# A recurrent attention loop that streams weights: one place and one block a step fewer

## The chip, the cores and the metric

The kernel runs on one core of a Trainium2 chip. Its engines work side by side, each through its own instruction stream: TensorE (PE for its matmuls, PEld for its weight loads), VectorE (DVE), ScalarE (ACT), GpSimd (POOL) and SyncE (SP), which here only issues DMAs. Sixteen DMA engines move data between HBM and the on-chip memory SBUF. The metric is the device time of one execution in microseconds. A time is the median of the runs shown.

## The reference

Two independent parts are computed and their outputs put side by side.

Part A is attention with a recurrent memory. The sequence of 2048 rows of 1024 is cut into 64 segments of 32. Each step joins the 8 memory rows with its 32 rows to `h` (40 rows), and computes with the same four weight matrices (1024 x 4096 each, bf16, 8 MB):

```
q, k, v = h Wq, h Wk, h Wv            # 32 heads of 128
p = softmax(q k^T * scale, masked)    # memory keys are seen by all; key j is allowed if j <= i, or i < 8
o = (p v) Wo
mem = o[:8];  out = o[8:]
```

`mem` is the input of the next step, so the steps run one after the other.

Part B is a long convolution by a state-space model: a kernel of 2048 taps for each of 1024 channels, from exponentials and cosines of 128 states, applied by a Fourier transform (in this kernel by matmuls with sine and cosine matrices), plus `u * Dskip`.

## The kernel before, in words

Part B comes first (0 to about 718 us of the profile). Beside it, part A's work that doesn't depend on the memory is done ahead: 24 rows of every segment are transposed and stored (`XTd`), and the projections of its last 8 rows are computed and stored (`PKd`). While B runs its table loop, SyncE also copies the weight blocks that will be streamed into DRAM tiles of their own (`streamed_copies`, tiles `WD_...`), and loads a first part of the weights that will stay.

Then comes part A's loop, `part_a`, 64 steps over `s` (line 339). The four matrices are 64 blocks of 128 x 2048 (512 KB each): `(m, t, kc)` for k, q and v, with half `t` of the heads and row block `kc` of 0 to 7, and `("o", u)` with `u` of 0 to 15 for Wo. They don't all fit in SBUF:

- *resident* blocks (`RESIDENT`) are loaded once and stay,
- two blocks (`KEPT`) lie in PSUM, and VectorE copies them from there to SBUF in five pieces each every step (`fetch`, L282),
- the blocks of `STREAM` and `STREAM_O` are *streamed*: loaded again each step, into one of `SLOTS` places in turn (`unit`, line 254, load at L268, tile `wst`).

`unit(key)` is called in the order in which TensorE uses the blocks, and it writes the load of a streamed block into SyncE's queue at that point. What paces it is the place: load number n waits until TensorE has used the block of load n - SLOTS. SyncE works its queue strictly in order, so a waiting entry holds up all behind it. The other entries of a step are hung on a block by the dictionary `between`: `load_pk` (L312, what was computed ahead for this step), `load_xt` (L317, the rows of the next step), and the two stores of the step before (`stores`, L327 to `OLd`, L331 to the output).

TensorE's order in a step: k half 0, q half 0 (8 blocks each; L349, four matmuls a block), transposes L360, k half 1 in two halves, scores (L373 to L380), q half 1, v half 0, v half 1, the products with the probabilities (L417, L421), then Wo's 16 blocks (L448, eight matmuls a block) and the transposition of the new memory (L542), which VectorE copies into `hT` (L543). That copy begins the next step; its start is the zero of the "step's clock" in this text. ScalarE evicts (L355, L435, L361), VectorE does the softmax and the block-diagonal spreading of the probabilities (L387 to L406).

Two tiles share memory with others under one tag and make entries of SyncE's queue wait: `xt` has tag `F`, which `lb0b` has before it (read by TensorE at L421, in the product of half 0), and `pk` is used until the last L421 of a step.

In the first step, resident blocks that have no place yet are loaded by `unit` as they come up (`rest`, L223). After the last step, the rows that were left for later are multiplied by Wo once more (L571), for which the Wo blocks that are not resident are loaded again.

GpSimd's DMA descriptors lie in the first 4096 bytes of each SBUF partition (`SCRATCH`, line 1315), and `low_blocks` puts three resident blocks behind them.

Of the kernel before, what the change touches and what calls it, by code (L numbers as in the profile page):

```python
# [21 lines left out]

STREAM = {("k", 0): (1,), ("q", 0): (0, 6), ("k", 1): (3,), ("q", 1): (0, 5), ("v", 0): (2, 7), ("v", 1): (2, 7)}
STREAM_O = (4, 7, 10, 14)

KEPT = {("k", 0, 7): (("B", 0, 512), ("C", 512, 512), ("A", 1024, 512), ("F", 1536, 256), ("L", 1792, 256)),
        ("o", 15): (("B", 0, 512), ("C", 512, 512), ("E", 1024, 512), ("F", 1536, 256), ("L", 1792, 256))}
SLOTS = 5  # L30


def weight_blocks(Wq, Wk, Wv, Wo):
# [15 lines left out]
def streamed_keys():  # L49
    return [key for key in [(m, t, kc) for (m, t), kcs in STREAM.items() for kc in kcs] + [("o", u) for u in STREAM_O]]  # L50

# [175 lines left out]
def part_a(ctx, tc, x, src, WD, HE, seg_len, out_a, ahead, W_res, rest, places, first):  # L227
# [20 lines left out]

    loads = [SLOTS]


    between = {}

    def unit(key):
# [9 lines left out]
        if key in first:  # L264
            return first.pop(key)
        t_ = wst.tile([128, 2048], BF16, name="wst", tag="w%d" % (loads[0] % SLOTS))
        loads[0] += 1
# [13 lines left out]
    def words(out, in_):  # L281
        nc.vector.tensor_scalar(out=out.bitcast(I32), in0=in_.bitcast(I32), scalar1=0, scalar2=None, op0=ALU.bitwise_or)  # L282

    def load_kept(key):
        i = len(kept)
        if key in first:
            t_ = first.pop(key)
        else:
            t_ = wst.tile([128, 2048], BF16, name="wst", tag="w%d" % (loads[0] % SLOTS))
            loads[0] += 1  # L290
            nc.sync.dma_start(out=t_[:].rearrange("e (h d) -> e h d", h=2) if key[0] == "o" else t_[:], in_=src(key))
        kept[key] = [ps_k.tile([128, 512], F32, name="keep", tag="keep%d" % (2 * i + n)) for n in range(2)]
        for n in range(2):
            words(kept[key][n][:], t_[:, 1024 * n:1024 * n + 1024])

    def fetch(key):

        ahead_of[key] = []
        for tag, lo, n in KEPT[key]:
            t_ = work.tile([128, n], BF16, name="piece", tag=tag)  # L300
            words(t_[:], kept[key][lo // 1024][:, lo % 1024 // 2:(lo % 1024 + n) // 2])
            ahead_of[key].append((lo, n, t_))
# [7 lines left out]
    def load_pk(j):  # L310
        pk = pers.tile([128, 768], BF16, name="pk", tag="pk")
        nc.sync.dma_start(out=pk[:], in_=PKd[j])  # L312
        return pk
# [12 lines left out]
    def stores(s, ob):  # L326
        nc.sync.dma_start(out=OLd[s // 8][:, 256 * (s % 8):256 * (s % 8) + 256], in_=ob[:, 1, :])  # L327
        rows = out_a[s * SL:s * SL + SL, :].rearrange("r (q d) -> q r d", q=4)
        if s + 1 < NS:

            nc.sync.dma_start(out=rows, in_=ob[:, 0, :])  # L331
        else:
            for q in range(4):
                nc.sync.dma_start(out=rows[q][0:XM], in_=ob[32 * q:32 * q + XM, 0, :])

    load_kept(("k", 0, 7))
    fetch(("k", 0, 7))
    between["v", 0, 2] = lambda: load_kept(("o", 15))
    for s in range(NS):
        def quads(m, t, kcs, a=None):  # L340
            if a is None:

                pool, tag = {("q", 0): (ps_sc, "sc"), ("q", 1): (ps_pv, "pv")}.get((m, t), (ps_acc, "acc"))
                a = pool.tile([128, 512], F32, name="acc", tag=tag)
            for kc in kcs:
                w = unit((m, t, kc))
                for g in range(4):
                    for o_, rhs in columns(w, 512 * g, 512):
                        nc.tensor.matmul(a[32 * g:32 * g + 32, o_:o_ + rhs.shape[1]], lhsT=hT[:, kc, :], rhs=rhs,  # L349
                                         start=(kc == 0), stop=(kc == KC - 1), tile_position=(0, 32 * g), skip_group_check=True)  # L350
            return a
# [101 lines left out]


        pks = []
        between["q", 0, 6] = lambda: pks.append(load_pk(s))
        if s:
            between["q", 1, 0] = lambda: stores(s - 1, ob)
        a = quads("k", 0, range(KC))
        k0 = evac(a, "A")  # L460
        a = quads("q", 0, range(KC))
# [73 lines left out]
        ob = work.tile([128, 2, 256], BF16, name="ob", tag="E")  # L535
# [801 lines left out]
def kernel(  # L1337
# [34 lines left out]
    def residents(stay, early):  # L1372
# [26 lines left out]
        for _ in range(EARLY[1]):  # L1399
            load_resident(tc, pool, src, rest.pop(0), W_res)  # L1400
            yield
        for i, key in enumerate([("k", 0, 7)] + streamed_keys()[0:SLOTS - 1]):
            first[key] = t_ = ahead.wst.tile([128, 2048], BF16, name="wst", tag="w%d" % i)
# [25 lines left out]
    with ExitStack() as ctx_a:  # L1429
        part_a(ctx_a, tc, A_x[0], src, WD, A_Wo.shape[0] * A_Wo.shape[1], seg_len, out_a, ahead, W_res, rest, places, first)  # L1430
# [35 lines left out]
```

## Time and profile before

| | us |
|---|---|
| median of 3 runs (2254.4 to 2264.52) | 2254.61 |
| the profiled execution: its own time | 2254.61 |
| its span | 2252.9 |
| part A's loop, first L349 to last L448 | 718.6 to 2190 |
| mean distance of two copies into hT (63 of them) | 22.6 |
| TensorE busy in the span | 1965.9 (87%) |
| VectorE busy | 1466.7 (65%) |
| DMA share and rate, 900 to 2100 us | 0.93 to 0.94, 342 to 349 GB/s |

In profile lines, L268 is line 268 of the kernel. A line of a group gives line, engine, operation, tiles (written<-read), shapes and count, then busy time and mean; a line of waits gives who waited for whom, microseconds in all, times and the longest. SPq is SyncE's queue: an entry there is the issue of a DMA, not its transfer. The ends of matmuls are modelled and a little late, so that matmuls seem to overlap, and a wait of less than about 0.2 us doesn't show.

### The profile page before, as it was taken

To read this page: it belongs to the slowest core of one execution; us is meant where nothing else is said; L and a number is where in the kernel's file an instruction comes from. 1 tells how busy PE (TensorE), PEld (TensorE's weight loads), DVE (VectorE), ACT (ScalarE), POOL (GpSimd) and SP (SyncE) were. 2 spreads that over 40 slices of the span, in tenths; PEclk is the share of its full clock that TensorE was granted. 3 is DMA by queue.
4 is the path that set the end of the run, shared out by engine and by line. 5 is a ranking of instruction groups with operands and counts; after the bars stand their busy time and mean duration, and the time that the engine had idled before them with its cause. 6 is when DMAs were issued, how large, how long until landed. Compare 5 with 4: busy or idle time off the path is not lost.

```text
span 2252.9 us, 77860 instructions
## 1 busy us (share of the span) xinstructions
PE 1965.9 (87%) x33798; PEld 1174.4 (52%) x33798; DVE 1466.7 (65%) x3160; ACT 976.3 (43%) x1599; POOL 359.5 (16%) x623
## 2 busy tenths in 40 slices
PE   1699999879999788989989898999998988999889
PEld 1365666657887344444444444544444444444444
DVE  8599999989995456565656565656565656565640
ACT  6699999932323233333333333333333333333330
POOL 2154444556222000000000000000000000000020
PEclk9999999989999899999999999999999999999999
DMA  6777886667459999999999999999999999999991
GB/s 161 194 197 228 226 238 180 176 178 243 156 180 318 345 329 335 349 335 355 323 346 345 347 340 354 345 355 333 355 337 356 332 356 330 355 342 360 333 377 37
DMA packets 351883, 657.84 MB, mean 292 GB/s; under 512 B 118616, under 2 KB 209912, under 8 KB 349492
## 3 DMA queue, kind: packets, MB, share of 16 engines
q1 hardware_dynamic: 336324, 608.69, 77.3%
q0 software_dynamic: 15216, 44.18, 5.8%
q8 instruction: 264, 4.33, 0.8%
q14 instruction: 79, 0.65, 0.1%
HBM read 597.97 MB, written 66.31 MB: 295 GB/s over the span
## 4 chain that ended last, share of the span: by engine, by line
PE 35%; DVE 24%; DMA 23%; issue 9%; ACT 6%; SPq 2%; POOL 1%; DVEq 0%; ACTq 0%; POOLq 0%
PE acc L349 16%; DMA wst<-WD_q 12%; DMA wst<-WD_o 5%; PE pe L571 3%; PE tr L360 3%; PE pro L158 2%; DVE nr L1068 2%; DMA out_dram<-uu 2%; PE ups L866 2%; DVE sc L388 2%; DVE sc L395 2%; DVE mx L393 2%; PE pp L448 2%; DVE pt L397 2%; PE pa L1037 2%
## 5 line engine op out<-in xcount | busy, mean ns | idle before, releaser
L349 PEld LDWEIGHTS <-hT 128*32 128x32 bf16 x12352 | 322.8, 97 | 323.6 <-issue 107.0
L355 ACT CAST ev<-acc 128x512 bf16<-128x512 f32 x384 | 224.8, 585 | 347.1 <-PE acc L349 341.1
L349 PE MATMUL acc<-W,hT 128*32 128x512 bf16 x4864 | 370.7, 381 | 0.0
L349 PE MATMUL acc<-wst,hT 128*32 128x512 bf16 x2560 | 257.7, 384 | 17.7 <-DMA wst<-WD_q 14.4
L448 PEld LDWEIGHTS <-oT 128*32 128x32 bf16 x8192 | 202.5, 96 | 111.2 <-issue 85.0
L282 DVE TENSOR_SCALAR piece<-keep 128x256 int32<-128x256 int32 (+1 forms) x640 | 188.9, 360 | 40.1 <-PE pp L448 31.3
L349 PE MATMUL acc<-MF,hT 128*32 128x512 bf16 x2048 | 182.4, 383 | 0.0
L448 PE MATMUL pp<-W_o,oT 128*32 128x256 bf16 x4096 | 159.2, 275 | 14.0 <-DMA W_o<-in_A_Wo_dram 5.6
L368 POOL COPY KT<-pk 128x128 bf16<-128x128 bf16 x128 | 37.7, 294 | 828.6 <-PE acc L349 372.0
L361 DVE COPY KT<-tr 128x512 bf16<-128x512 bf16 x64 | 27.2, 424 | 215.1 <-PE tr L360 215.1
L387 DVE TENSOR_REDUCE mx<-sc 128x8 f32<-128x320 f32 x128 | 62.1, 485 | 159.3 <-PE sc L380 159.3
L435 ACT CAST oT<-pv 128x512 bf16<-128x512 f32 x128 | 75.0, 586 | 165.1 <-PE pv L421 162.6
L448 PE MATMUL pp<-wst,oT 128*32 128x256 bf16 x2048 | 102.6, 277 | 26.6 <-DMA wst<-WD_o 25.9
L158 PE MATMUL pro<-xTl,wsl 128*128 128x512 bf16 x512 | 120.2, 386 | 5.2 <-ACT xTl L102 5.2
L361 ACT COPY QT<-tr 128x512 bf16<-128x512 bf16 x128 | 75.0, 586 | 109.5 <-PE tr L360 107.9
L389 ACT ACTIVATE sc<-sc 128x320 f32<-128x320 f32 x128 | 54.0, 422 | 156.6 <-DVE sc L388 150.3
L1007 PEld LDWEIGHTS <-MF 128*128 128x128 bf16 x1024 | 102.6, 100 | 29.9 <-issue 8.5
L360 PEld LDWEIGHTS <-ev 128*128 128x128 bf16 x1024 | 57.9, 97 | 110.0 <-issue 80.6
L321 POOL COPY hT<-xt 128x192 bf16<-128x192 bf16 x63 | 21.9, 347 | 562.3 <-DMA xt<-XTd 473.9
L1007 PE MATMUL hps<-KT,MF 128*128 128x256 bf16 x720 | 94.3, 284 | 14.4 <-DVE x L1182 11.4
L1239 PE MATMUL yp<-Bt,MI 128*128 128x256 bf16 x680 | 102.8, 273 | 0.8 <-ACT yb L1255 0.8
L538 ACT CAST ob<-pp 128x128 bf16<-128x128 f32 x64 | 17.0, 265 | 197.8 <-DVE ob L537 197.8
(314 smaller groups left out, 3962.2 us busy)
## 6 DMA issues: line engine op xcount, KB each, us to landing
wst<-WD_q SPq DMA_DIRECT2D x256, 512.0 KB
wst<-WD_v SPq DMA_DIRECT2D x256, 512.0 KB
wst<-WD_o SPq DMA_DIRECT2D x256, 512.0 KB
wst<-WD_k SPq DMA_DIRECT2D x128, 512.0 KB
Ud<-ux POOLq DMA_DIRECT2D x16, 1024.0 KB, 5.6
uq<-Ud SPq DMA_DIRECT2D x32, 512.0 KB
pk<-PKd SPq DMA_DIRECT2D x64, 192.0 KB
wsl<-in_A_Wk_dram SPq DMA_DIRECT2D x16, 512.0 KB
```

What stands on the lines that cost most here:

```text
L158: nc.tensor.matmul(a[:], lhsT=w[:, kc, 128 * j:128 * j + 128], rhs=xTl[:, kc, :, :].rearrange("p s k -> p (s k)"), start=(kc == 0), stop=( ...
L282: nc.vector.tensor_scalar(out=out.bitcast(I32), in0=in_.bitcast(I32), scalar1=0, scalar2=None, op0=ALU.bitwise_or)
L349: nc.tensor.matmul(a[32 * g:32 * g + 32, o_:o_ + rhs.shape[1]], lhsT=hT[:, kc, :], rhs=rhs, start=(kc == 0), stop=(kc == KC - 1), tile_pos ...
L355: nc.scalar.copy(out=q[:], in_=a[:])
L360: nc.tensor.transpose(out=p[:, i, hl, :, :].rearrange("p a b -> p (a b)"), in_=q[:, 128 * hl:128 * hl + 128], identity=ident[:])
L361: eng(out=dst, in_=p[:, i, :, :, :])
L387: nc.vector.tensor_reduce(out=mx[:], in_=sc, axis=AX.X, op=ALU.max)
L435: nc.scalar.copy(out=o[:], in_=p[:].rearrange("p a (g q) -> p a g q", g=4))
L448: nc.tensor.matmul(po[32 * qt:32 * qt + 32, :], lhsT=oT[:, h % 4, (h % 16) // 4, :], rhs=columns(w, 1024 * hh + 256 * qt, 256)[0][1], star ...
L571: nc.tensor.matmul(pe[n][:], lhsT=left[2 * b + hi // 16][:, 128 * (hi % 16):128 * (hi % 16) + 128], rhs=wo[u][:, 1024 * hh + 512 * n:1024 ...
L1007: pe.matmul(s_[r][half][:, cs, :], lhsT=MF[:, kc, 4 * rr + mc, cs, :], rhs=rhs, start=(i == 0 and mc == 0), stop=(i == 1 and mc == 3), ski ...
L1239: pe.matmul(yp[:, b, :], lhsT=m_[:, b, cs, kc, :], rhs=Bt[:, kc, j, half, c_, :], start=(kc == 0 and cs == 0 and half == 0), stop=(kc == 3 ...
```

## The change

One place fewer for streamed blocks (four for five), and one block fewer streamed in a step (13 for 14), which becomes resident. Which blocks are streamed is chosen anew, and with that the places at which the other entries of SyncE's queue are hung. `SCRATCH`, `low_blocks` and all arithmetic stay.

```
-STREAM = {("k", 0): (1,), ("q", 0): (0, 6), ("k", 1): (3,), ("q", 1): (0, 5), ("v", 0): (2, 7), ("v", 1): (2, 7)}
-STREAM_O = (4, 7, 10, 14)
+STREAM = {("k", 0): (1,), ("q", 0): (1, 7), ("k", 1): (4,), ("q", 1): (1,), ("v", 0): (0, 4), ("v", 1): (0, 5)}
+STREAM_O = (3, 7, 10, 14)
...
-SLOTS = 5
+SLOTS = 4
...
-    between["v", 0, 2] = lambda: load_kept(("o", 15))
+    between["v", 0, 0] = lambda: load_kept(("o", 15))
...
-        between["q", 0, 6] = lambda: pks.append(load_pk(s))
+        between["q", 0, 7] = lambda: pks.append(load_pk(s))
         if s:
-            between["q", 1, 0] = lambda: stores(s - 1, ob)
+            between["k", 1, 4] = lambda: stores(s - 1, ob)
```

SyncE's queue over one step, from the load of xt on:

```
before: xt, o10, o14, k0.1, q0.0, pk, q0.6, k1.3, stores, q1.0, q1.5, v0.2, v0.7, v1.2, v1.7, o4, o7
after:  xt, o10, o14, k0.1, q0.1, pk, q0.7, stores, k1.4, q1.1, v0.0, v0.4, v1.0, v1.5, o3, o7
```

(q0.6 is block 6 of q, half 0; from k0.1 on they are for the next step.)

## The prediction

> **What bounds the kernel now.** I read the page first, for the stage in which the change lies. Slices are 56.3 us wide; the attention recurrence runs from about 719 us (first L349) to 2190 us.
>
> ```profile
> span 2252.9 us, 77860 instructions
> ...
> DMA  6777886667459999999999999999999999999991
> GB/s 161 194 197 228 226 238 180 176 178 243 156 180 318 345 329 335 349 335 355 323 346 345 347 340 354 345 355 333 355 337 356 332 356 330 355 342 360 333 377 37
> ...
> PE 35%; DVE 24%; DMA 23%; issue 9%; ACT 6%; SPq 2%; POOL 1%; DVEq 0%; ACTq 0%; POOLq 0%
> ```
>
> The DMA engines look full from slice 13 on, and DMA is 23% of the chain that ended last. That would make every megabyte less a gain. But a share of busy time is not a wait, so I asked next what TensorE itself waits for between 770 and 2160 us, some 62 steps that are alike (the view of waits, PE alone):
>
> ```profile
> PE tro L542 <- DVE ob L537: 27.4, 61, 0.5
> PE acc L349 <- DVE hT L543: 22.9, 61, 0.4
> PE pp L448 <- DMA wst<-WD_o: 18.9, 31, 1.6
> ...
> PE acc L349 <- DMA wst<-WD_q: 14.1, 33, 0.9
> ...
> PE acc L349 <- DMA wst<-WD_k: 2.3, 7, 0.6
> PE acc L349 <- DMA wst<-WD_v: 0.2, 1, 0.2
> ```
>
> Columns: microseconds in all, times, longest. Weights cost TensorE 18.9+14.1+2.3+0.2 = 35.5 us there, 0.57 us of a 22.6 us step (63 copies into hT, L543, from 760.8 to 2164.4 us). The rest is instruction stream and the turn of the state (L542, L543), which the change leaves alone. Then what SyncE's DMA queue waits for, in the same stretch, and one step of that queue in order of time:
>
> ```profile
> SPq L317 <- PE pv L421: 217.7, 62, 3.9
> SPq L327 <- ACT ob L545: 114.5, 61, 3.2
> SPq L312 <- PE pp L421: 100.7, 61, 2.1
> ```
>
> ```profile
> 1525.65 0.32 SPq L317 DMA_DIRECT2D xt<-XTd  x1
> 1526.02 1.82 SPq L268 DMA_DIRECT2D wst<-WD_o  x2
> 1527.94 0.39 SPq L268 DMA_DIRECT2D wst<-WD_k  x1
> 1528.42 0.38 SPq L268 DMA_DIRECT2D wst<-WD_q  x1
> 1530.21 0.32 SPq L312 DMA_DIRECT2D pk<-PKd  x1
> 1530.58 0.42 SPq L268 DMA_DIRECT2D wst<-WD_q  x1
> 1531.20 0.41 SPq L268 DMA_DIRECT2D wst<-WD_k  x1
> 1533.66 0.32 SPq L327 DMA_DIRECT2D OLd<-ob  x1
> 1534.03 0.55 SPq L331 DMA_DIRECT2D out_dram<-ob  x1
> 1534.67 1.11 SPq L268 DMA_DIRECT2D wst<-WD_q  x2
> ```
>
> Every step SyncE stands 217.7/62 = 3.5 us at the load of xt, which takes over the tile lb0b and so waits for L421 to have read it; Wo blocks 10 and 14 are queued behind. In this step the load before them landed at 1527.19 and theirs at 1530.67 and 1531.95 (the trace's landing records): between 1527.2 and the start of their packets the DMA engines run dry, some 2 us in every step. From there they work without a pause: landings 1.2 to 1.4 us apart at 1530.67, 1531.95, 1533.33, 1534.65, pk 1535.12. So what matters is not the bytes of a step but the chain that starts anew at xt. Where it is too late stands in TensorE's own timeline:
>
> ```profile
> 1531.99 0.40 PE L448 MATMUL pp<-wst,oT 128*32 128x256 bf16 x8 [0.19 <-DMA wst<-WD_o]
> ...
> 1537.50 0.40 PE L349 MATMUL acc<-wst,hT 128*32 128x512 bf16 x4 [0.27 <-DMA wst<-WD_q]
> 1537.71 0.40 PE L349 MATMUL acc<-MF,hT 128*32 128x512 bf16 x4
> ```
>
> The first is Wo block 14 (landed 1531.95), the second Wq block 6 of half 0 (landed 1537.45): they start 0.04 and 0.05 us after the landing.
>
> **The change part by part.** Times below are on a step's clock, zero at the copy into hT (1533.68 here), as medians of the 53 to 58 steps I could read whole.
>
> *Later places in q, half 0.* Streamed blocks 0 and 6 become 1 and 7. After xt the queue holds the same things in the same order: Wo 10, Wo 14, Wk 1, a Wq block, pk, a Wq block. Same bytes, so the last lands when it does now, at 3.8, and TensorE reaches it one block later: four matmuls, 0.22 us start to start (1537.71 less 1537.50 above is 0.21). A wait shrinks by 0.22 us at most; 33 waits of 14.1/33 = 0.43 us are mostly longer: 33 x 0.22 = 7.3 us. Taken from start to start (which also sees what the modelled ends hide) the wait is 0.37 us a step and would be 0.22: 0.15 x 63 = 9.5 us. I take 8.5. The first Wq block waits in one step in 58: 0.5 us at most. The later issue does no harm: block 1 goes out when Wo 7's place is free (-3.7), 6 us before its use at 2.3; block 7 when Wo 10's is (-2.5), 6.2 us before 3.7.
>
> *Wo.* Block 4 becomes 3, which feeds nothing that waits. Blocks 10 and 14 keep their place on TensorE and their place behind xt; with four places 14 also waits for the use of Wv 5 of half 1, over 0.5 us after L421, while SyncE comes to it 0.9 us or more after L421. Their 18.9 us stay: 0, bounds -18.9 and +10 (half as much again).
>
> *One block less a step, 14 to 13.* 1.3 us of DMA time. It goes missing in the stretch before xt, where the streamed v blocks and Wo 7 land 0.6 to 1.7 us before their use already; the dry time grows from 2 to about 3 us. 0. If it shortened the chain after xt, up to all of the remaining 35.5 us would go; that end goes to a rival.
>
> *Four places.* A load is now held back by the use four loads earlier. Laid out with today's block starts, the time from that use's end to the new block's use is 5.9 to 6.9 us, and 4.7 for Wo 10, which xt sets as now. A load that finds the engines idle took 1526.02 to 1530.67 = 4.65 us with a long issue, 4.1 in the median; one in a full queue 5.5 to 7.5. At one block per 1.69 us (22/13) against 1.3 us of transfer the queue drains between blocks, so 0; the one tight place comes next.
>
> *Stores moved ahead of Wk 4, half 1.* Today Wk 3 goes out before the two stores (1531.20). In the new order SyncE stands at the stores until ACT's copy L545 (-0.02), and Wk 4 goes out at 1.0 where Wq 0 of half 1 does now (1534.67). TensorE wants it at about 5.9 (Wk 3's median start 5.43, plus one transpose of 0.33 and two blocks less what was saved). Queued behind the late Wq 7 (3.8), the stores and its own 1.3 us it lands near 5.4: today's block there lands at 6.67 with Wk 3's 1.27 us more ahead of it. It is late in about 5 steps of 54; I take +2 us. Bounds: 0 (it lands 3.5 us after its issue, as Wo 10 does), and +47 us (it takes the 5.2 us after the end of its issue that today's block there takes, so lands at 6.64, 0.74 us late, 63 times).
>
> The trace has five landing records for each out_dram store and sixteen for each weight load. The Trainium skill, "DMA: Bandwidth & Descriptors", section "Why a DMA increments its semaphore by 16 and not by 1", says that a copy is spread over the largest count up to 16 that divides the slowest dimension of both sides; by it, with 4 column groups, the store sits on four engines, and Wk 4's share there stands behind 32 packets of 512 B instead of 8. At the trace's 27 ns a packet that is 0.65 us later, 6.05 instead of 5.4, and the sum would be some 10 to 15 us higher. Today's block after the same store lands 1.56 us after Wk 3, which leaves no room for it.
>
> *First step and the rest.* The list of resident blocks has 49 entries for 48; the loads before the loop are one streamed block fewer, those that the first step makes as it goes are 12 for 11. There SyncE issues block by block at 1.36 us (745.15 to 749.15, three and one) and TensorE stalls on each: +1.4 us. One copy fewer among the table work of the first stage, and the same five Wo blocks reloaded at the end: 0, within 2 us.
>
> **Sum:** -8.5 - 0.5 + 2 + 1.4 = -5.6 us. The profiled execution's own time is 2254.61 us (span 2252.9), equal to the median shown; so 2249.
>
> **Rivals.** *Both weight waits go.* If the chain after xt runs faster because fewer loads share the engines, the 33 (q) and 31 (Wo) waits vanish. For it: the block behind each is often late on one engine only. Against: the loads ahead are the same ones. Half of it, 2235; all, -35.5 + 1.4 with hidden parts, about 2215. *Slower: Wk 4 behind the stores.* Nothing hides it: it is used 4.9 us after its issue, and if it needs more than that the excess is paid 63 times. Loads at that place of the queue take 5.2 us after issue's end (4.3 to 5.6 for the middle 8 in 10). At 5.2, 2249 - 2 + 47 = 2294; at 4.8, about 2265. *It does nothing:* if Wq 7 also lands later by its place (it is issued half a microsecond later), the 8.5 us stay and the time is 2257; that lies in my own range.
>
> **How the numbers follow.** Small gain or nothing (2238 to 2258): 0.52. Waits go (2208 to 2238): 0.23. Wk 4 late, or four places too few elsewhere (2258 to 2305): 0.25. Leaving a tenth on either side: 2217 to 2288; the likeliest alone 2238 to 2258. Half a per cent, 11.3 us, is about what can be told from no change: below 2243.3 lie the second and a fifth of the first, 0.33; above 2265.9 most of the third, 0.23; between, 0.44.
>
> **What would show it.** Right: TensorE's wait for WD_q at about half of 14.1 us, for WD_o near 18.9, for WD_k under 5; the stall of L317 unchanged; the DMA share at about 0.88 for 0.93. Wrong: a wait for WD_k of tens of microseconds (the stores), waits for WD_v (four places), or WD_o's wait gone (the chain after xt was not what I took it for).

## The result and the profile after

The changed kernel takes 2296.4 us (median of four runs, 2295.36 to 2297.48), the kernel before 2256.81 in the same comparison (2254.4 to 2264.52). The ratio is 1.0169, 95% interval 1.0142 to 1.0196: slower by 40 us, where I had forecast 2249 and a range of 2217 to 2288. The profiled execution of the changed kernel has an own time of 2297.48 us, 42.9 more than the one of before.

From its page, the span, the two DMA rows of the 40 slices, and the shares of the chain that ended last:

```profile
span 2295.8 us, 77858 instructions
...
DMA  6777885666368988998899989899899899999991
GB/s 162 197 218 222 224 228 167 181 205 231 118 236 306 315 305 300 319 314 297 299 318 321 312 315 312 299 313 314 309 301 317 306 316 315 323 312 321 313 347 49
...
PE 42%; DMA 29%; DVE 11%; issue 8%; ACT 6%; SPq 1%; POOL 1%; ACTq 0%; DVEq 0%; POOLq 0%
```

In the loop (slices 13 to 37) the DMA engines move some 310 GB/s where they moved 345, and yet their share of the chain has grown from 23% to 29%. Fewer bytes, and TensorE waits for them longer. The view of waits, TensorE alone, 770 to 2200 us (the last copy into hT is now at 2207.5; columns are microseconds in all, times, longest):

```profile
PE pp L448 <- DMA wst<-WD_o: 29.3, 48, 1.9
PE tro L542 <- DVE ob L537: 27.3, 61, 0.5
PE acc L349 <- DVE hT L543: 22.9, 61, 0.4
PE acc L349 <- DMA wst<-WD_k: 22.0, 33, 1.7
...
PE acc L349 <- DMA wst<-WD_q: 12.0, 27, 1.2
...
PE acc L349 <- DMA wst<-WD_v: 1.0, 3, 0.4
```

The waits on the turn of the state (L542, L543) are what they were. The weights cost 64.3 us for 35.5: WD_k went from 2.3 to 22.0, WD_o from 18.9 to 29.3, and WD_q only from 14.1 to 12.0. SyncE's queue in the same stretch:

```profile
SPq L268 <- PE acc L349: 299.4, 327, 2.8
SPq L317 <- PE pv L421: 162.9, 62, 2.8
SPq L327 <- ACT ob L545: 135.8, 61, 3.6
```

It stands less long at xt (162.9 for 217.7 us), because it comes there later: with four places it has been held up by L268, the weight loads, before. All waits of the queue at L268, of which the first line is the largest, add up to 708 us, and to 475 in the kernel before (770 to 2160 us). One step of the queue and, below it, what TensorE does when Wk 4 of half 1 is due:

```profile
1535.92 0.98 SPq L268 DMA_DIRECT2D wst<-WD_q  x1
1538.02 0.32 SPq L327 DMA_DIRECT2D OLd<-ob  x1
1538.43 0.55 SPq L331 DMA_DIRECT2D out_dram<-ob  x1
1539.08 0.42 SPq L268 DMA_DIRECT2D wst<-WD_k  x1
1539.59 0.38 SPq L268 DMA_DIRECT2D wst<-WD_q  x1
```

```profile
1543.55 0.40 PE L360 MATMUL tr<-a_ident,ev 128*128 128x128 bf16 x4
1544.22 0.40 PE L349 MATMUL acc<-wst,hT 128*32 128x512 bf16 x4 [0.27 <-DMA wst<-WD_k]
1544.43 0.40 PE L349 MATMUL acc<-W,hT 128*32 128x512 bf16 x4
```

Wk 4 is issued behind the two stores, at 1539.08, and lands at 1544.18 by the trace's landing records; its first matmul starts 0.04 us later. In 29 of the 61 steps the profile shows a wait there (the other 4 of the 33 are at the first Wk block).

Where the 42.9 us came from, start to start, as means over the 59 steps that can be read whole (a step lasted 22.60 us before and 23.30 after, 0.70 more; over all 62 it is 0.67). From the first copy into hT to the last, 762.1 to 2207.5 us, are 1445.4 us, where 760.8 to 2164.4 were 1403.6: the loop has 41.7 of the 42.9 us, and 1.4 were lost before the first copy (0.2 less were spent behind the last).

| place in the step | us a step against before |
|---|---|
| Wq 6 became Wq 7, half 0 | -0.17 |
| first Wq block, half 0 | +0.07 |
| Wk 4, half 1 | +0.37 |
| Wq 1, half 1 | +0.08 |
| Wo 10 | +0.10 |
| Wo 14 | +0.15 |
| matmuls at half clock, about | +0.1 |

### The profile page after: what moved, and what is told of

Same layout as the page of the kernel before. It is cut to its first block, busy times and chain, and to the rows that moved or that the text cites. A ratio compares the mean times of both kernels' runs of the same rounds, so it can differ in the third digit from the quotient of the medians.

```text
span 2295.8 us, 77858 instructions
## 1 busy us (share of the span) xinstructions
PE 1979.5 (86%) x33798; PEld 1187.1 (52%) x33798; DVE 1467.0 (64%) x3160; ACT 976.1 (43%) x1599; POOL 359.5 (16%) x623
## 4 chain that ended last, share of the span: by engine, by line
PE 42%; DMA 29%; DVE 11%; issue 8%; ACT 6%; SPq 1%; POOL 1%; ACTq 0%; DVEq 0%; POOLq 0%
PE acc L349 23%; DMA wst<-WD_o 11%; DMA wst<-WD_k 9%; DMA wst<-WD_q 4%; PE pp L448 3%; PE tr L360 2%; PE pe L571 2%; PE pro L158 2%; DVE nr L1068 2%; DMA out_dram<-uu 2%; PE ups L866 2%; PE pa L1037 2%; DMA KT<-Kd 2%; ACT ev L355 1%; DMA wst<-WD_v 1%
## 5 line engine op out<-in xcount | busy, mean ns | idle before, releaser
L349 PEld LDWEIGHTS <-hT 128*32 128x32 bf16 x12352 | 333.7, 97 | 349.1 <-issue 135.5
L349 PE MATMUL acc<-W,hT 128*32 128x512 bf16 x5120 | 373.2, 382 | 1.2 <-DMA W<-in_A_Wv_dram 1.2
L349 PE MATMUL acc<-wst,hT 128*32 128x512 bf16 x2304 | 234.0, 389 | 50.7 <-DMA wst<-WD_k 22.0
L448 PEld LDWEIGHTS <-oT 128*32 128x32 bf16 x8192 | 204.4, 97 | 127.7 <-issue 101.0
L282 DVE TENSOR_SCALAR piece<-keep 128x256 int32<-128x256 int32 (+1 forms) x640 | 188.9, 360 | 48.2 <-PE pp L448 33.4
L448 PE MATMUL pp<-W_o,oT 128*32 128x256 bf16 x4608 | 176.2, 278 | 15.8 <-DMA W_o<-in_A_Wo_dram 7.6
L349 PE MATMUL acc<-MF,hT 128*32 128x512 bf16 x2048 | 158.6, 381 | 0.0
L448 PE MATMUL pp<-wst,oT 128*32 128x256 bf16 x2048 | 103.6, 279 | 36.1 <-DMA wst<-WD_o 35.2
L1007 PEld LDWEIGHTS <-MF 128*128 128x128 bf16 x1024 | 102.9, 101 | 29.3 <-issue 8.8
```

The costliest lines, as they stand in the source:

```text
L448: nc.tensor.matmul(po[32 * qt:32 * qt + 32, :], lhsT=oT[:, h % 4, (h % 16) // 4, :], rhs=columns(w, 1024 * hh + 256 * qt, 256)[0][1], star ...
L1007: pe.matmul(s_[r][half][:, cs, :], lhsT=MF[:, kc, 4 * rr + mc, cs, :], rhs=rhs, start=(i == 0 and mc == 0), stop=(i == 1 and mc == 3), ski ...
```

## The experiments

The change has two parts that could each explain this. P: four places hold too few loads in flight. S: the stores ahead of Wk 4 make that load late. A third thing, the dry stretch behind xt that both kernels have, was tried as well (theory A of the expectations from e5 on: the load of xt holds up what is queued behind it; B is its rival there). "A step" below is the mean start-to-start time of a step against the 22.60 us of before, from the run's one profiled execution; the medians are of all its executions.

### The stores moved back behind Wk 4 (e1_stores_later)

```
-            between["k", 1, 4] = lambda: stores(s - 1, ob)
+            between["q", 1, 1] = lambda: stores(s - 1, ob)
```

> The changed kernel with the two stores hung on Wq 1 of half 1, so that Wk 4 of half 1 goes out ahead of them (queue: pk, q0.7, k1.4, stores, q1.1). Theory S (Wk 4 is late because its issue stands behind the stores, at 1.04 us of the step): the wait for WD_k goes from 22.0 us to under 4 us, and the kernel to 2255 to 2272. Theory P (four places are too few; Wk 4 would be late anyway, as its place comes free only with Wo 14, and the lateness moves to the next block): 2285 to 2300, with the lost wait found again at WD_q or WD_v.

Measured against the kernel after, whose change it undoes in part: 2277.99 us (2269.24 to 2286.04), ratio to before 1.0094 (1.0063 to 1.0125); a step +0.40 for +0.70. TensorE's waits, 770 to 2160 us:

```profile
PE pp L448 <- DMA wst<-WD_o: 30.6, 49, 1.8
...
PE acc L349 <- DMA wst<-WD_q: 9.0, 25, 1.0
PE acc L349 <- DMA wst<-WD_k: 5.3, 8, 1.3
```

The wait for WD_k has all but gone, so Wk 4 was late because the stores stood ahead of it. But 0.40 of the 0.70 stays, and the wait for WD_o is as large as in the kernel after. The time lies between the ranges of the two theories: S explains three sevenths by the steps, and 19 of the 40 us by the medians.

### Five places again, all else as changed (e2_five_places)

The fifth place is paid for with a resident block that is left out: half 1 of v multiplies by its block 6 a second time in place of block 7, so that all instructions stay, but this part of the result is not the reference's. (Its line numbers are two higher: L351 is L349, L450 is L448.)

```
-SLOTS = 4
+SLOTS = 5
...
+        if key == ("v", 1, 7):
+            key = ("v", 1, 6)
```

> The changed kernel with five places; the room is made by leaving out resident block v, half 1, kc 7 (kc 6 is used twice, so this block's product is not computed, but as many matmuls run). Same streamed blocks, same queue order, stores still ahead of Wk 4. Theory S: no better than 2285, since Wk 4 still waits for the stores. Theory P: 2250 to 2265, and waits for weights about as in the kernel before.

Measured: 2245.51 us (2238.94 to 2252.82), ratio 0.9958 (0.9931 to 0.9986); a step -0.12. TensorE's waits:

```profile
PE acc L351 <- DMA wst<-WD_k: 15.0, 26, 1.3
PE pp L450 <- DMA wst<-WD_o: 12.7, 25, 1.1
...
PE acc L351 <- DMA wst<-WD_q: 3.9, 12, 0.4
```

Giving back the place is worth 0.82 us a step and takes the waits for WD_o and WD_q down together, which P said, though the time is below P's range too. WD_k stays late (0.25 us a step at Wk 4 for 0.37), with the stores still ahead of it. P is the larger of the two.

### The kernel before with four places (e3_before_four_places)

```
-SLOTS = 5
+SLOTS = 4
```

> The kernel before with four places for five and nothing else (14 blocks streamed). Theory S: up to 2275, some blocks a little later. Theory P: 2290 or more, with waits for weights spread over several blocks.

Measured: 2322.74 us (2319.93 to 2331.3), ratio 1.0283 (1.0226 to 1.034); a step +1.18, of which Wo 10 has +0.79, Wo 14 +0.20, block 2 of v, half 1, +0.15.

```profile
PE pp L448 <- DMA wst<-WD_o: 65.6, 92, 2.9
PE acc L349 <- DMA wst<-WD_v: 7.4, 14, 1.1
```

One line alone makes the kernel before slower than the whole change does. The waits are not spread over several blocks, as P had it, but lie for the most part at Wo 10. Waits for WD_v, which I had named as the sign of four places, do appear here; in the kernel after, whose streamed blocks lie elsewhere, the sign is in WD_o.

### The kernel before with the stores ahead of Wk 3 (e4_before_stores_early)

```
-            between["q", 1, 0] = lambda: stores(s - 1, ob)
+            between["k", 1, 3] = lambda: stores(s - 1, ob)
```

> The kernel before with the stores hung on Wk 3 of half 1, so that they stand ahead of it as in the change. Theory S: Wk 3 goes out at 1.0 us of the step for a use at 5.0 to 5.4, late by 0.5 us and more each step: 2280 to 2300, WD_k waits of 20 to 40 us. Theory P: within 2250 to 2265.

Measured: 2307.91 us (2303.88 to 2317.07), ratio 1.0227 (1.0175 to 1.028); a step +0.99: Wk 3 +0.52, Wq 0 and 5 of half 1 +0.15 and +0.12, Wo 14 +0.22.

```profile
PE pp L448 <- DMA wst<-WD_o: 27.5, 44, 1.6
PE acc L349 <- DMA wst<-WD_k: 24.5, 36, 1.6
PE acc L349 <- DMA wst<-WD_q: 22.4, 36, 2.2
```

Here P's forecast was wrong and S right in kind, with a time above its range: with five places the stores cost 0.99 us a step where the block behind them is used one block sooner. The late load itself is half of that; the rest is at three more loads behind it in the queue. That their lateness is handed on from the first is likely, but was not tested by itself.

### xt behind Wo 14 (e5_after_xt_behind, e6_before_xt_behind)

The load of xt waits for its tile, and Wo 10 and Wo 14 are queued behind it; here they go first. Once in the kernel after, once in the kernel before, with the same edit:

```
-            between["o", 10] = lambda: put_xt(load_xt(s + 1))
-        oproj(pp[:, 1, :], range(8, 14), o1)
+        oproj(pp[:, 1, :], range(8, 15), o1)
+        if s + 1 < NS:
+            put_xt(load_xt(s + 1))
         fetch(("o", 15))
-        oproj(pp[:, 1, :], range(14, 16), o1)
+        oproj(pp[:, 1, :], (15,), o1)
```

> The changed kernel with the load of xt moved in SyncE's queue from ahead of Wo 10 to behind Wo 14 (no other edit). Theory A (what four places cost at Wo 10 and 14, and a part of what follows, comes from the chain that starts anew at xt): waits for WD_o from 28 us to under 8 us and the time to 2240 to 2265; Wk 4 stays late (its issue at 1.04 us is the stores'). Theory B (with four places the blocks arrive late because each waits for a use four loads back, xt or not): WD_o keeps more than 18 us, 2280 to 2296.

> The same move of xt in the kernel before (five places, 14 blocks). Theory A: the dry 2 us of every step go, waits for WD_o and WD_q from 33 us to under 10 us, 2205 to 2230. Theory B's counterpart (the five places are all taken by then, so nothing goes out earlier): 2245 to 2260.

The kernel after so changed: 2280.19 us (2275.2 to 2283.28), ratio 1.0127 (1.0083 to 1.0171); a step +0.40 for +0.70. Its waits:

```profile
PE acc L349 <- DMA wst<-WD_k: 26.0, 30, 3.2
...
PE acc L349 <- DMA wst<-WD_q: 11.8, 19, 1.5
PE pp L448 <- DVE piece L282: 10.2, 28, 0.6
PE pp L448 <- DMA wst<-WD_o: 3.3, 9, 1.2
```

The wait for WD_o fell from 28.2 (same window) to 3.3, as A had it, and the time is the one that B gave: part of the gain is lost at the pieces of Wo 15 (L282, +0.51 us a step), one of which is copied into the tile that xt uses before it, and at Wk 4, where a step now loses 0.47 for 0.37.

The kernel before so changed: **2216.2 us** (2215.03 to 2219.39), ratio 0.9851 (0.9811 to 0.9891). It beats both kernels. A step is 0.59 us shorter: Wo 14 -0.38, the second Wq block -0.27, the first Wk block -0.08, against +0.18 at the pieces and +0.11 at each streamed Wq block of half 1. Its waits, and one window of 350 us in this kernel (window, its length, then busy times with counts of TensorE, its weight loads, VectorE, ScalarE and GpSimd, the granted clock, DMA share, GB/s):

```profile
PE acc L349 <- DMA wst<-WD_q: 9.6, 18, 1.3
PE pp L448 <- DMA wst<-WD_o: 4.5, 4, 2.0
PE pp L448 <- DVE piece L282: 2.4, 8, 0.4
```

```profile
1110.00:1460.00 350.00, 321.34 (x6767) 173.40 (x6763) 206.65 (x571) 122.53 (x239) 15.08 (x48) 1.00 0.98 353
```

The same window in the kernel after:

```profile
1110.00:1460.00 350.00, 309.65 (x6382) 166.89 (x6379) 193.62 (x541) 115.37 (x225) 14.04 (x45) 0.98 0.90 311
```

All 14 blocks a step, at 353 GB/s. By the packet records the share of the time in which fewer than four DMA engines are at work is 0.000, in the kernel before 0.039. The two waits of its view come to 14.1 us for 33, not to under 10 as A had it, and the time is in A's range. So the hole behind xt was worth 36 us, and it could be closed without one byte less.

### xt between Wo 10 and Wo 14 (e9_before_xt_between)

```
-            between["o", 10] = lambda: put_xt(load_xt(s + 1))
-        oproj(pp[:, 1, :], range(8, 14), o1)
+            between["o", 14] = lambda: put_xt(load_xt(s + 1))
+        oproj(pp[:, 1, :], range(8, 15), o1)
         fetch(("o", 15))
-        oproj(pp[:, 1, :], range(14, 16), o1)
+        oproj(pp[:, 1, :], (15,), o1)
```

> The kernel before with the load of xt between Wo 10 and Wo 14 in SyncE's queue (e6 had it behind both, at 2216 us, and xt then came late for the last piece of Wo 15, 0.18 us a step). If only Wo 10 has to get past xt to fill the dry stretch, this keeps e6's gain without that new wait: 2200 to 2216. If Wo 14 is then late as before: 2225 to 2245.

Measured: 2234.3 us (2232.01 to 2240.38), ratio 0.9905 (0.987 to 0.994); a step -0.25. Half of the gain: Wo 14, still behind xt, gains 0.09 us a step where it gained 0.38.

### What a place is worth without the hole (e10_before_xt_behind_four)

The kernel before with xt behind Wo 14 and `SLOTS = 4`.

> e6 (the kernel before with xt behind Wo 14) with four places for five. If a place is worth what it was with xt ahead (e3 against before: 1.18 us a step), 2275 to 2300; if most of that was the chain that starts at xt, 2225 to 2250.

Measured: 2325.93 us (2322.48 to 2330.59), ratio 1.0314 (1.0273 to 1.0355); a step +1.10, or 1.69 more than with five places.

```profile
PE pp L448 <- DVE piece L282: 21.8, 58, 0.6
PE pp L448 <- DMA wst<-WD_o: 20.1, 43, 1.7
```

Both forecasts were too low. With four places and 14 blocks a step takes 23.7 to 23.8 us wherever xt stands (e3 and this one): four places turn over 14/4 = 3.5 times in a step, so once in 6.8 us. In this run the places pace the queue: each load is issued within 0.1 us of the last use of its place (means by block), and 5.1 of the 6.8 us pass from the end of its issue to its landing. But a block then lies ready for 0.9 us in the mean before TensorE uses it, so it is not shown that 6.8 us is the shortest possible turn. The loss against the kernel before is for the most part at the pieces of Wo 15 (+0.77 us a step), as in e5.

### Both orders mended in the kernel after, and with five places (e7_after_both_moved, e8_five_places_stores_later)

The first is the kernel after with xt behind Wo 14 and the stores on `between["q", 1, 1]`; the second the five-place kernel with the stores there, and with the same block of v left out.

> The changed kernel with xt behind Wo 14 and the stores behind Wk 4 of half 1. If stores and xt cost independently of one another, the gains add: e1's 0.30 us a step and that of the run with xt moved alone, 2225 to 2250 by theory A, 2262 to 2280 by theory B.

> The run with five places (one resident block left out, v, half 1, kc 7) and the stores behind Wk 4 too. With five places Wk 4 was still late by 0.25 us a step behind the stores; if that is the stores' alone it goes, and the time is 2225 to 2236. If the lateness passes on to the next block: 2240 to 2250.

The first: 2252.58 us (2239.26 to 2259.75), ratio 0.9999 (0.9966 to 1.0031); a step -0.12. The two gains of 0.30 add up, with 0.22 more (0.82 in all); and the kernel is then where it was before the change. The second: 2225.11 us (2213.29 to 2236.62), ratio 0.9888 (0.9834 to 0.9942); a step -0.21 in its profiled execution, which is the slowest of its four. The wait at Wk 4 is gone, so with five places too it was the stores. The first time is between the two forecasts, the second at the low end of the one for the stores alone.

The four corners of the two parts, as steps against before:

| | 13 blocks (choice of after) | 14 blocks (choice of before) |
|---|---|---|
| 5 places, stores behind | -0.21 | 0 |
| 5 places, stores ahead | -0.12 | +0.99 |
| 4 places, stores behind | +0.40 | +1.18 |
| 4 places, stores ahead | +0.70 (the change) | not run |

A single execution can mislead: e2's profiled one is the fastest of its ten, e8's and e3's the slowest of their four. The differences of the medians to those of before, by 62 steps, are -0.45 and -0.20 (five places, e8 and e2) and +0.33 and +0.64 (four places) in the first column, +0.81 (e4) and +1.05 (e3) in the second. The order is the same.

## Why the prediction was wrong, point by point

**Four places: 0.** This is the step that failed most. The fifth place is worth 0.82 us a step with the stores ahead and 0.61 with them behind, some 51 and 38 us in 62 steps (51 and 48 by the medians). I had laid windows of 5.9 to 6.9 us beside a load "that finds the engines idle", 4.1 to 4.65 us from the start of its issue, and had noted "one in a full queue 5.5 to 7.5" in the same sentence. The first was the wrong row, and the truth lies between the two: in the kernel after, loads in mid-step land 4.4 to 5.7 us after the end of their issue (medians by block; the 90th percentiles reach 5.3 to 6.6), or 4.8 to 6.1 from its start. From the last use of a place to the start of its next use are 6.2 to 7.8 us there (means by block). That still leaves most blocks ready 0.5 to 1.8 us early; it leaves least, 0.4 us and less, where SyncE stands before the issue as well: at Wk 4 (2.3 us, the stores) and at Wo 10 and 14 (1.6 and 0.6 us, xt). The loads ahead of these go out later than with five places, when a place comes free, and are then still in flight: with the same blocks Wo 7 is issued 12.0 us into the step for 10.1 in e2 (five places), and lands 1.1 us after the end of Wo 10's issue for 0.1.

Of the reason I gave, "the queue drains between blocks", the draining is seen, but not that it is free: at least 16 packets were being moved at once for 0.56 of the time after, for 0.74 before, and packets of 4 KB took 187 ns in the mean for 174. So 13 blocks kept the DMA engines busy 19.48 us of a step, where 14 had kept them busy 19.47 (18.3 for 13 blocks with five places, e2). The engines' work did not shrink with the block that went. The term had no bounds, only its 0, and the 0.25 on "Wk 4 late, or four places too few elsewhere" ended at 2305 because of the other half of that rival.

**Stores moved ahead of Wk 4: +2, bounds 0 to +47.** Measured 0.30 us a step, 19 us, within its bounds. The price failed in the landing: 6.04 us after the copy into hT in the median of 62 steps for my 5.4 (issued at 1.04, as worked out; end of issue 1.46, then 4.55 us). I had taken Wk 3's 1.27 us off the landing of today's block there, 6.67; 0.63 came off. Its due time was also off: the median use is at 6.50, 5.54 at the earliest, late itself through the waits before it. The bound of 6.05 by the Trainium skill, "DMA: Bandwidth & Descriptors", section "Why a DMA increments its semaphore by 16 and not by 1" (the store on four engines only), was closer than mine; five landing records of each store agree with it, but loads elsewhere in the step are as slow with four places, and the last four of Wk 4's sixteen records come 1.04 us behind the twelfth here and 0.84 in e1, where the stores are behind it: a difference of 0.2 us for the 0.65. So these runs do not show that the stores' packets are what delays Wk 4's share.

**Later places in q, half 0: -8.5.** Right: -0.17 us a step, -10.5 us, for -0.15. The wait of the view fell by only 2.1 us for all that, because it also holds Wq 1 of half 1 (+0.08 a step, behind the late Wk 4) and the first block (+0.07). The sign I gave, "about half of 14.1", was a bad one: a sum over three places.

**Wo: 0, bounds -18.9 and +10.** Measured +0.25 us a step for Wo 10 and 14, some 15 us; in the wait 10.4, so just outside. Wo 14 is issued at the same time behind xt, but xt itself lands 2.71 us after its issue's end for 1.82, Wo 14 5.08 for 4.34: with four places the dry stretch no longer lies ahead of them. I had read "some 2 us" of dryness in every step and had it grow to about 3. By the packet records fewer than four engines were at work for 0.9 us of a step before (in the step shown from 1527.2 to 1528.1), and for 0.3 after (shares 0.039 and 0.014): half of what I had read, and it shrank. The stall of L317, which I held unchanged, fell by 55 us. This is the four places again: with five, Wo 14 is 0.07 us a step sooner than before.

**One block less a step: 0.** With five places and the stores behind, the 13 blocks of the new choice gain 0.21 us a step in e8's profiled execution and 27.6 us by its median, 0.45 a step; 0.17 of that is the q gain. So 0.04 to 0.28 a step, 2 to 17 us, are left for the block, and 0 was at the low end. That was with five places; that its time goes missing in the dry stretch, as I had it, did not happen with four, where that stretch shrank.

**First step: +1.4.** The number is right by luck: the first copy into hT is 1.4 us later, made of 1.4 us gained before the loop (first L349 at 717.2 for 718.6; in the other runs it lies between 716.7 and 720.0) and 2.8 lost in the first step, twice my price. (The four issues from 745.15 to 749.15 lie 1.33 us apart, not 1.36.)

**The rivals.** "Wk 4 behind the stores" gave 2294, and the time came out at 2296, but for the most part by the other mechanism; its sign, a WD_k wait of tens of microseconds, was there (22.0). That it is only three sevenths is what e1 and e2 tell. "Both weight waits go" had the right thing to go, and the wrong means: e6 got to 2216, near its 2215, by moving xt.

## What to carry to other kernels

Count loads in flight, not bytes: the time between two uses of a place must hold the wait of the queue, the issue and the landing of a load, and the row for that is a load in mid-stream, not one behind a dry stretch. Here, with 512 KB blocks, a block less a step did not pay for the fifth place (more than five were not tried). Before bytes are cut, look for an entry of the DMA queue that waits for its tile with loads behind it: moving one of 48 KB behind two weight loads gave 1.5%.

## What the runs showed of the hardware

With four places the packets themselves are slower. The 4 KB packets took 174 ns in the mean in the kernel before, 176 and 177 in e2 and e6 and 184 to 187 in the kernels with four places; packets over 300 ns were 3.0% before and 5.7% after. What slows them is open. With four places more of them start while only 8 to 13 of the 16 engines are at work: 238 a step in the kernel after, 91 before.

Short waits that add up to some 1.5 us can be enough for a stretch at half clock. Four windows of the kernel after, two stretches and what stood ahead of each (columns as in the windows above):

```profile
1067.10:1070.50 3.40, 1.82 (x34) 1.00 (x37) 1.36 (x5) 0.54 (x2) 0.00 (x0) 0.99 0.97 367
1070.50:1073.90 3.40, 3.40 (x41) 1.67 (x37) 0.50 (x3) 0.58 (x1) 0.29 (x1) 0.51 0.72 245
...
1090.90:1094.30 3.40, 1.90 (x38) 0.88 (x31) 1.56 (x6) 0.54 (x2) 0.00 (x0) 1.00 1.00 387
1094.30:1097.70 3.40, 3.40 (x37) 1.74 (x33) 0.31 (x2) 0.37 (x1) 0.29 (x1) 0.51 0.93 311
```

In each pair TensorE is busy 1.8 to 1.9 of 3.4 us, and for the next 3.4 us the granted clock is half: 37 to 41 matmuls, where the 3.4 us from 1073.9 on have 60. The waits ahead are 1.7, 0.4 and 0.4 us in the first pair, and 0.4, 0.4, 0.4 and 0.2 in the second. Not every such stretch does it: from 1042.1 to 1045.5 us TensorE is busy 1.46 us, and the clock stays at 1.00 in it and in the 3.4 us behind it. The Trainium skill, "TensorE: Matmul & The Clock Gate", "Part 1: The HAM clock gate", has a window of about 3.4 us, which agrees (the stretches at half clock last 3.4 or 6.8 us), and lets the clock fall after an idle window; here one that was a little under half idle was enough. The clock was at half for 37.5 us of the 59 steps after, 13.7 before, 71.7 in e3 and 0.0 in e6. A wait so costs more than its length where it gathers with others at the turn of a step.

It was not tried to give xt a tile of its own (384 B a partition), so that its load would have no L421 to wait for and Wo 15's pieces no xt.
